# Threshold attention and a SwiGLU block: the first planned slots, six products by blocks and the order of the last jobs

## Chip, cores and metric

One Trainium2 chip, one of its cores. The metric is the device time of one execution in microseconds (us). The kernel before was timed three times: 1342.71, 1343.5 and 1345.19, median 1343.5.

The core's engines run side by side, each through its own queue in order: TensorE (PE; PEld is its weight load), VectorE (DVE), ScalarE (ACT) and GpSimd (POOL). SyncE (SP) issues the DMA transfers.

## What is computed

Attention with a threshold, over 8 batches of 8 heads, 576 tokens and 64 columns a head, and then a SwiGLU block on the 4608 tokens by 512 columns that come out of it. All is fp32.

```python
scores = scale * np.matmul(q, k.transpose(0, 1, 3, 2))
thresh = np.max(scores, axis=-1, keepdims=True) - tau
scores = np.where(scores >= thresh, scores, -1000000000.0)
scores = scores - np.max(scores, axis=-1, keepdims=True)
attn = np.exp(scores)
attn = attn / (np.sum(attn, axis=-1, keepdims=True) + 1e-09)
x = np.matmul(attn, v)            # then (batch, seq, heads * 64) -> (4608, 512)
...
g = x @ w_gate                    # w_gate, w_val: 512 x 1536
silu = g * (1.0 / (1.0 + np.exp(-g)))
return silu * (x @ w_val) @ w_out # w_out: 1536 x 512
```

## The kernel before

**Chunks.** The 4608 tokens are nine chunks of 512: c = 0 to 7 hold the first 512 tokens of each batch, c = 8 (`B` in the code) the last 64 tokens of all batches. A chunk's gate and value are made in groups g of the columns of d_ff, each group by a Strassen-Winograd scheme: seven products p1 to p7 of half-sized matrices in place of eight, with sums of weights and sums of x made beforehand, and the products joined afterwards by sums on DVE, POOL and ACT. From chunk `DEEP` = 2 on, the output product (by w_out) is done by the same scheme on two levels (class `Deep`).

**By blocks.** A flat product is eight rows of PE's record, each 128x128 weights against 256 columns. By blocks (`NestedGroup`, L1321) it is split once more into seven block products of 128 columns, 14 rows, which need sums of x (`deepen_x`, L1305), an emptying of two banks (`Seven.fill`, L1271 and L1273) and a fold of four sums (`Seven.fold`, L1276). Groups 1, 2 and 3 of chunks 3 to 6 have two such products each, p5 and p3 (`FOLDS`, `WITH_BLOCKS`).

**Attention in slots.** After a prologue with batch 0, which ends near 129 us, the heads of batches 1 to 7 run in 84 slots s, 12 to a batch: batch b holds slots 12(b−1) to 12b−1, and kk is the number of the slot in its batch, from 0. A slot makes the scores of two heads for a third of the tokens (`slot_scores`, L2058), and `slot_rest` does the rest: row maxima on DVE (L2079, L2081), exchanged between groups of partitions by DVE (L2087) or by ACT, the negative maximum (L2088, L2097), the threshold on ACT (L2100), six exponentials on ACT (L2104), six masks with sums on DVE (L2106), the exchange of the sums on ACT (L2115), total and reciprocal on DVE (L2120, L2121), six scalings on ACT (L2133) or POOL (L2130), and three transposes on DVE (L2135). PE's next scores reuse the banks that the masks read. Every third slot ends with attend (L2157), the product by v, which waits for the transposes. Tables say which slots do a job where: `FIRST_MAX_BY_ACT` and `FIRST_POOLED` by s for batches 1 and 2, `MAX_BY_ACT` and `POOLED` by kk for the others.

**Between scores and attend** PE does other work, so many steps a slot by tables: `PLAIN` in batch 1 (the rest of chunks 0 and 1, without Strassen sums of weights; L1371), `GV` for the gates and values of chunk b−1 during batch b, `CD` and `CH` for output products. PE's order is thus written out by hand. The weights' last pieces, w_out, come in during the first slots: SP loads them, ACT splits them (L953, L956), DVE and POOL join them (`rest_of_weights`).

**The planner.** The order of DVE, ACT, POOL and SP comes from a list scheduler (class `Plan`). Each job has an engine, a duration that the code gives it (`took`), jobs it waits for, a `lag` added for its readers and a rank. Whenever an engine is free by the plan, it takes the ready job of lowest rank; -1 goes ahead of 0. The engines then run the order so found, whatever the real times are: a job that waits longer than planned holds up those behind it.

**Tail.** After the last scores (near 1110 us) no slots are left. Chunks 7 and 8 run group by group in turn (class `Whole`, from L2526; PE rows at L2543), every product by blocks; `finish` gives the tanh (L2593) and the gated sums (L2595), L2615 and L2625 empty p3 and p7 onto earlier products. Chunk 8's gated sums are stored to HBM (L2608) and loaded back at its output product (L2669). The output product of chunk 7 starts inside the last group: its sums are `early`, `sums_of_last`, `late` (all of whole blocks, through `sum`), and `inner_sums` (o) for the product o of seven, of four sums j3, j1, j2, j4 that wait for each other. `gates_end` is the step that ends the last group and calls `late` if nobody did. `p7_alone` uses the sixth inner sums. L929 and L926 are the helpers by which all sums on DVE and on POOL are recorded, L1768 and L1777 PE rows of output products, L2018 and L2020 emptying into sums, L1829 and L1642 stores of outputs and loads of weight sums.

Of the kernel before, what the change touches and what calls it, by code (L numbers as in the profile page):

```python
# [14 lines left out]
ALU = mybir.AluOpType  # L15
# [129 lines left out]
def kernel(  # L145
# [27 lines left out]
    NU3 = 3  # L173
# [1087 lines left out]
    class Seven(Buf):  # L1261
# [13 lines left out]
        def fold(self, eng, rank, *deps):  # L1275
# [7 lines left out]
            return job(eng, took, tt(y[:, 4:6], twice(6), y[:, 4:6], ALU.add), j, rank=rank)  # L1283
# [391 lines left out]
    class Deep:  # L1675
# [57 lines left out]
        def sum(self, out, a, b, op, x, *deps, rank=2):  # L1733
# [3 lines left out]
            if self.by_pool and not self.in_outputs:  # L1737
                tt, eng, took = pool_tt, "POOL", 1.3
            return job(eng, took, tt(out[:, fs], a[:, fs], b[:, fs], op), *deps, rank=rank)

        def inner_sums(self, o, a, place, ready, *deps):
# [5 lines left out]
            rank = 0 if o == 1 and self.c == B - 1 else 0 if o == 1 else 1 if o == 5 or o in (3, 6) and not tail[0] or o in (0, 6) and tail[0] or self.c == B - 2 else 2  # L1747
# [315 lines left out]
    def slot_rest(seg, t, pss, mark, pooled, max_by_act, rank):  # L2063
# [53 lines left out]
        xj = job("ACT", 0.78, exchange, *masks.values(), rank=1)  # L2117
# [5 lines left out]
        rj = job("DVE", 0.36, total, xj, rank=1)  # L2123
# [102 lines left out]
    def gates_and_values(c):  # L2226
# [5 lines left out]
        for g in range(NF2):  # L2232
            deep = c > DEEP and g in WITH_BLOCKS
# [59 lines left out]
    def block_part(b, kk):  # L2293
# [17 lines left out]
        if kk in GV:  # L2311
            if kk == 1:
                state["gv"], state["c"] = gates_and_values(c), c
                if c > DEEP:
                    deepen_x(c, *(j for js in streamed_kept.values() for j in js))
# [7 lines left out]
            if c == DEEP and kk <= len(NESTED):  # L2323
                deepen(NESTED[kk - 1], plan.t, *(j for js in plain_stores.values() for j in js), *summed)
# [13 lines left out]
    for s, (n, x) in enumerate((n, x) for n in range(len(halved)) for x in range(NU3)):  # L2338
# [6 lines left out]
        if s == 0:  # L2345
# [5 lines left out]
            plan.free.update(DVE=2.0, ACT=2.5)  # L2351
# [10 lines left out]
        at_, pooled, max_by_act = (kk, POOLED, MAX_BY_ACT) if b > DEEP else (s, FIRST_POOLED, FIRST_MAX_BY_ACT)  # L2362
# [273 lines left out]
    for g in range(NF2):  # L2636
        for c in (B - 1, B):
# [10 lines left out]
            for fn in (new.p2, new.p6, new.p3, new.p7) if old is not None else (new.p5, new.p2, new.p6, new.p3, new.p7):  # L2648
# [3 lines left out]
                if (c, g) == (B, NF2 - 1) and fn == new.p6:  # L2652
                    state["deep"].late(plan.t + plan.PIPE)
# [59 lines left out]
```

## Time and profile before

| | |
|---|---|
| median of three runs | 1343.5 us |
| the profiled execution, whole | 1344.29 us |
| its span on the core | 1342.4 us |
| granted clock of TensorE | 0.999 |
| PE, DVE, ACT, POOL busy | 99%, 81%, 67%, 69% |
| 16 DMA engines, kernel's own queue | 52.2% |
| HBM read, written | 169.08 MB, 38.01 MB |

Times are read from the span's start. In the views, "idle" in brackets is how long the engine stood still before a row, and the arrow names what it waited for. "x4" is so many instructions taken together, and the duration beside it is from the start of the first to the end of the last. PE's rows overlap: a row's duration is longer than the distance to the next, so PE's pace is read from start to start.

### The profile page before, as it was taken

Reading aid. Unit: us, or ns where it says so; the run is one execution under the profiler, and the core shown is the slowest. Engines: PE = TensorE matmul, PEld = TensorE weight load, DVE = VectorE, ACT = ScalarE, POOL = GpSimd, SP = SyncE. Lnnn points to the kernel's source line nnn. Section 1 sums busy time; section 2 is a strip of 40 time slices with the busy share of each in tenths; the row PEclk is TensorE's granted clock in tenths of the full one; section 3 lists DMA queues with packets and bytes.
Section 4 is the critical chain, followed back from the end, with each engine's and each line's share of the span. In section 5 each row is a group of like instructions: output and inputs, shape, how many; then the busy total and the mean of one; then the engine's idle time right before and its main releaser. Section 6 shows DMA issues by size and latency. Waiting matters only on the chain. (4 is left out here: it accounts for less than half of the span.)

```text
span 1342.4 us, 41686 instructions
## 1 busy us (share of the span) xinstructions
PE 1327.0 (99%) x16274; PEld 1123.1 (84%) x16274; DVE 1082.9 (81%) x2891; ACT 899.1 (67%) x2341; POOL 932.8 (69%) x1115
## 2 busy tenths in 40 slices
PE   9999999999999999999999999999999999999998
PEld 7777877787887878888888888888888889999998
DVE  7888898888887778888888887888888887667886
ACT  6888777767756677787777777777777775344300
POOL 2688497565685759857895779677976799856720
PEclk9999999999999999999999999999999999999999
DMA  8852424356557553656365746655474627565241
GB/s 180 205 188 92 85 58 134 122 150 178 154 166 220 174 167 89 208 165 219 76 201 168 232 111 187 178 168 149 115 214 146 213 68 232 158 202 183 88 169 40
DMA packets 230884, 209.81 MB, mean 156 GB/s; under 512 B 167968, under 2 KB 185376, under 8 KB 223008
## 3 DMA queue, kind: packets, MB, share of 16 engines
q1 hardware_dynamic: 226768, 206.22, 52.2%
q8 instruction: 129, 2.11, 0.7%
q10 hardware_dynamic: 3920, 0.92, 0.3%
q14 instruction: 67, 0.55, 0.1%
HBM read 169.08 MB, written 38.01 MB: 154 GB/s over the span
## 5 line engine op out<-in xcount | busy, mean ns | idle before, releaser
L2106 DVE SCALAR_TENSOR_TENSOR pall<-sc,th,pall 128x288 f32<-128x288 f32 x504 | 244.2, 513 | 42.6 <-ACT pall L2104 23.4
L2104 ACT ACTIVATE pall<-sc,nm 128x288 f32<-128x288 f32 x504 | 232.9, 498 | 35.3 <-DVE pall L2106 34.9
L2135 DVE STREAM_TRANSPOSE pall<-pall 128x576 f32<-128x576 f32 x252 | 188.3, 764 | 22.1 <-ACT pall L2133 12.1
L1138 PE MATMUL pb<-xall,big 128*128 128x256 f32 x864 | 205.8, 381 | 0.0
L2133 ACT ACTIVATE pall<-pall,ri 128x288 f32<-128x288 f32 x388 | 178.9, 527 | 27.7 <-DVE ri L2121 26.9
L926 POOL TENSOR_TENSOR big<-big 128x128 f32<-128x128 f32 (+3 forms) x214 | 158.9, 751 | 46.5 <-ACT big L1273 20.8
L1138 PEld LDWEIGHTS pb<-xall,big 128*128 128x128 f32 x864 | 161.2, 190 | 24.0 <-issue 2.2
L926 POOL TENSOR_TENSOR hall<-hall,tmp 128x512 f32<-128x512 f32 x80 | 102.3, 1279 | 95.6 <-DVE hall L1197 75.9
L2079 DVE TENSOR_REDUCE mx<-sc 128x2 f32<-128x576 f32 x168 | 125.7, 748 | 39.7 <-PE sc L2058 39.3
L2058 PE MATMUL sc<-kT,qT 64*32 64x288 f32 (+1 forms) x5376 | 145.3, 345 | 0.4 <-DVE pall L2106 0.4
L1138 PE MATMUL pa<-xall,big 128*128 128x256 f32 x576 | 137.7, 382 | 0.0
L2058 PEld LDWEIGHTS sc<-kT,qT 64*32 64x32 f32 x5376 | 96.2, 106 | 48.6 <-issue 9.3
L2157 PE MATMUL xa<-pall,vall 64*32 64x288 f32 x4032 | 129.4, 404 | 0.5 <-PE px L1768 0.4
L1138 PEld LDWEIGHTS pa<-xall,big 128*128 128x128 f32 x576 | 107.8, 190 | 17.5 <-issue 2.5
L2157 PEld LDWEIGHTS xa<-pall,vall 64*32 64x32 f32 x4032 | 75.6, 107 | 46.6 <-issue 5.0
L2130 POOL TENSOR_SCALAR pall<-pall,ri 128x288 f32<-128x288 f32 x116 | 58.2, 513 | 53.1 <-DVE ri L2121 52.8
L1138 PE MATMUL pe<-xall,big 128*128 128x256 f32 x384 | 91.4, 381 | 0.0
L2115 ACT COPY sums<-sums 32x6 f32<-32x6 f32 x336 | 66.6, 198 | 30.3 <-DVE pall L2106 25.2
L1138 PEld LDWEIGHTS pe<-xall,big 128*128 128x128 f32 x384 | 72.4, 190 | 11.1 <-ACT pall L2133 0.7
L2081 DVE TENSOR_REDUCE mx<-sc 128x1 f32<-128x288 f32 x168 | 75.0, 447 | 0.0
L926 POOL TENSOR_TENSOR hall<-hall 128x384 f32<-128x384 f32 (+2 forms) x69 | 70.0, 1028 | 0.8
L1196 ACT ACTIVATE vall<-tmp 128x512 f32<-128x512 f32 x72 | 45.1, 627 | 35.6 <-POOL tmp L926 19.0
(365 smaller groups left out, 3051.6 us busy)
## 6 DMA issues: line engine op xcount, KB each, us to landing
big<-sums_hbm SPq DMA_DIRECT2D x30, 1280.0 KB, 7.9
big<-sums_hbm SPq DMA_DIRECT2D x30, 1024.0 KB, 7.8
vall<-in_v_dram SPq DMA_DIRECT2D x112, 144.0 KB, 3.5
big<-sums_hbm SPq DMA_DIRECT2D x54, 256.0 KB, 3.6
sums_hbm<-big SPq DMA_DIRECT2D x36, 256.0 KB, 3.8
out_dram<-big SPq DMA_DIRECT2D x32, 256.0 KB, 2.8
qT<-in_q_dram SPq DMA_DIRECT2D x112, 72.0 KB, 4.0
kT<-in_k_dram SPq DMA_DIRECT2D x112, 72.0 KB, 3.0
```

The source lines that it names most:

```text
L926: return lambda: nc.gpsimd.tensor_tensor(out=out, in0=a, in1=b, op=op)
L1138: nc.tensor.matmul(ps[:, i], w[:, k_, i * P:(i + 1) * P], x[:, k_, :], start=first and i == k_ == 0, stop=True, skip_group_check=True)
L2058: nc.tensor.matmul(pss[h][(slice(g * G, (g + 1) * G), *part)], qT[hs, col:col + G], kT[hs, c * SH + keys[0]:c * SH + keys[1]], start=True, ...
L2079: rs.append(job("DVE", 0.72, lambda n=n, tile_=tile_: nc.vector.tensor_reduce(out=mx[:, n:n + 2, 0], in_=tile_[:, :, 0:SH], axis=AX.X, op= ...
L2081: rs.append(job("DVE", 0.42, lambda n=n, tile_=tile_: nc.vector.tensor_reduce(out=mx[:, n + 2:n + 3, 0], in_=tile_[:, :, SH:SH + SQ], axis ...
L2104: ej = job("ACT", 0.42, lambda x=x, n=n: nc.scalar.activation(ps[x], scs[x], AF.Exp, bias=nm[:, n:n + 1]), ej, masks.get((h, u - 1)), rank=0)
L2106: masks[x] = job("DVE", 0.45, lambda x=x, n=n: nc.vector.scalar_tensor_tensor(out=ps[x], in0=scs[x], scalar=th[:, n:n + 1], in1=ps[x], op0 ...
L2115: nc.scalar.copy(sm[g * G:(g + 1) * G, 0:m, 1], sm[o * G:(o + 1) * G, 0:m, 0])
L2130: scaled.append(job("POOL", 0.48 if seg["i"] >= 3 * NP else 0.4, lambda x=x, n=n: nc.gpsimd.tensor_scalar(out=x, in0=x, scalar1=ri[:, n:n ...
L2133: scaled.append(job("ACT", 0.46, lambda x=x, n=n: nc.scalar.activation(x, x, AF.Copy, scale=ri[:, n:n + 1]), rj, rank=rank))
L2135: seg["turned"].append(job("DVE", 0.72, lambda both=both: nc.vector.transpose(out=both, in_=both), *scaled, rank=rank))
L2157: nc.tensor.matmul(holds[a].ap()[x * G:(x + 1) * G, 0:SH].rearrange("d (i q) -> d i q", q=G), vr[rs, h, j, ds], p[rs, h, :, j, :], start=( ...
```

## The change

Six edits, all of order or place except the fourth, which replaces products:

1. `rest_of_weights`: the first load of a w_out piece is planned to land 7.6 us in, before 6.3; ACT is planned free 4.4 us into slot 0, before 2.5.
2. `FIRST_POOLED`, `FIRST_MAX_BY_ACT`: which slots of batches 1 and 2 have scalings on POOL and maxima exchanged by ACT. ACT exchanges the maxima in 10 slots, before 12.
3. `PLAIN`: one step of PE's work goes from slot 2 to slot 3.
4. Chunk 2 joins the chunks whose groups 1, 2 and 3 do p5 and p3 by blocks; the three `deepen` calls (sums for two-level output products) of that batch go from kk = 1 to 3 to kk = 4 to 6.
5. The last slot of all: exchange and total at rank -1, and two scalings on POOL.
6. Tail: each fold's last sum is planned with a lag of 0.6; `late` is called from `gates_end` and not after p6 of the last group, and its sums and the one of `second_of_s1` go to DVE, since the switch `by_pool` is gone; first inner sums have rank 1 in the tail except for chunk 7's, sixth ones of chunk 8 rank 0.

```diff
@@ rest_of_weights
-        landed = 6.3
+        landed = 7.6
@@ Seven.fold
-            return job(eng, took, tt(y[:, 4:6], twice(6), y[:, 4:6], ALU.add), j, rank=rank)
+            return job(eng, took, tt(y[:, 4:6], twice(6), y[:, 4:6], ALU.add), j, rank=rank, lag=0.6 if tail[0] else 0.0)
@@ Deep
-        by_pool = False
-
         def second_of_s1(self):
-            self.by_pool = True
@@ Deep.sum
-            if self.by_pool and not self.in_outputs:
-                tt, eng, took = pool_tt, "POOL", 1.3
@@ Deep.inner_sums
-            rank = 0 if o == 1 and self.c == B - 1 else 0 if o == 1 else 1 if o == 5 ...
+            rank = 0 if o == 6 and self.c == B else 0 if o == 1 and self.c == B - 1 else 1 if o == 1 and tail[0] else 0 if o == 1 else 1 if o == 5 ...
@@ slot_rest
-        xj = job("ACT", 0.78, exchange, *masks.values(), rank=1)
+        first = -1 if seg is halved[-1] and t == seg["tiles"][-1] else 1
+        xj = job("ACT", 0.78, exchange, *masks.values(), rank=first)
...
-        rj = job("DVE", 0.36, total, xj, rank=1)
+        rj = job("DVE", 0.36, total, xj, rank=first)
@@ gates_and_values
-            deep = c > DEEP and g in WITH_BLOCKS
+            deep = c >= DEEP and g in WITH_BLOCKS
@@ tables
-    POOLED = {0: 3, 1: 1, 2: 1, 3: 3, 4: 3, 5: 2, 6: 1, 7: 2, 8: 1}
+    POOLED = {NS: 2, 0: 3, 1: 1, 2: 1, 3: 3, 4: 3, 5: 2, 6: 1, 7: 2, 8: 1}
-    FIRST_POOLED = {0: 2, 4: 1, 5: 1, 8: 1, 9: 1, 11: 2, 12: 2, 13: 3, 15: 3, 16: 3, 17: 2, 19: 2, 20: 2, 22: 3, 23: 3}
-    FIRST_MAX_BY_ACT = (1, 3, 6, 9, 10, 11, 12, 13, 14, 18, 20, 21)
+    FIRST_POOLED = {0: 2, 4: 2, 5: 1, 6: 1, 8: 2, 10: 1, 11: 2, 12: 2, 13: 3, 16: 3, 17: 2, 18: 1, 19: 1, 20: 3, 22: 3, 23: 3}
+    FIRST_MAX_BY_ACT = (1, 2, 3, 6, 9, 11, 12, 14, 15, 21)
-    PLAIN = {0: 3, 1: 5, 2: 6, 3: 2, 4: 5, 5: 5, 6: 3, 7: 3}
+    PLAIN = {0: 3, 1: 5, 2: 5, 3: 3, 4: 5, 5: 5, 6: 3, 7: 3}
@@ block_part
-                if c > DEEP:
+                if c >= DEEP:
                     deepen_x(c, *(j for js in streamed_kept.values() for j in js))
-            if c == DEEP and kk <= len(NESTED):
-                deepen(NESTED[kk - 1], ...)
+            if c == DEEP and 4 <= kk < 4 + len(NESTED):
+                deepen(NESTED[kk - 4], ...)
@@ slots
-            plan.free.update(DVE=2.0, ACT=2.5)
+            plan.free.update(DVE=2.0, ACT=4.4)
-        at_, pooled, max_by_act = (kk, POOLED, MAX_BY_ACT) if b > DEEP else (s, FIRST_POOLED, FIRST_MAX_BY_ACT)
+        at_, pooled, max_by_act = (kk if n + 1 < len(halved) or x + 1 < NU3 else NS, POOLED, MAX_BY_ACT) if b > DEEP else (s, FIRST_POOLED, FIRST_MAX_BY_ACT)
@@ tail groups
-                if (c, g) == (B, NF2 - 1) and fn == new.p6:
-                    state["deep"].late(plan.t + plan.PIPE)
```

More of the change, by code (lines that the diff above doesn't have):

```diff
@@ L1746, in inner_sums @@
             tt, eng, took = (dve_tt, "DVE", 0.55) if tail[0] else (pool_tt, "POOL", 1.0)
-            rank = 0 if o == 1 and self.c == B - 1 else 0 if o == 1 else 1 if o == 5 or o in (3, 6) and not tail[0] or o in (0, 6) and tail[0] or self.c == B - 2 else 2
+            rank = 0 if o == 6 and self.c == B else 0 if o == 1 and self.c == B - 1 else 1 if o == 1 and tail[0] else 0 if o == 1 else 1 if o == 5 or o in (3, 6) and not tail[0] or o in (0, 6) and tail[0] or self.c == B - 2 else 2
             j3 = job(eng, took, tt(s3, a11, a21, ALU.subtract), *ready, *deps, rank=rank)
@@ L2322, in block_part @@
                     last_of_streamed(o, plan.t)
[L2323 to L2324 removed]
+            if c == DEEP and 4 <= kk < 4 + len(NESTED):
+                deepen(NESTED[kk - 4], plan.t, *(j for js in plain_stores.values() for j in js), *summed)
             if kk == LAST_GV:
```

## The prediction

> **What bounds the kernel now.** The page's first part was read first: busy time by engine.
>
> ```profile
> PE 1327.0 (99%) x16274; PEld 1123.1 (84%) x16274; DVE 1082.9 (81%) x2891; ACT 899.1 (67%) x2341; POOL 932.8 (69%) x1115
> ```
>
> TensorE (PE) is busy in 1327.0 of 1342.4 us, at a granted clock of 0.999. Nothing can be won but its 15.4 us of idle time, the time its matmuls are stretched by a wait inside a run, and matmul work itself. So the second view is the waits of PE, after the prologue (which the change leaves alone):
>
> ```profile
> PE sc L2543 <- DVE tmp L2625: 0.9, 1, 0.9
> PE px L1768 <- DVE big L929: 0.9, 1, 0.9
> ...
> PE sc L2543 <- ACT tmp L1273: 0.5, 1, 0.5
> PE xa L2157 <- PE px L1768: 0.4, 1, 0.4
> PE sc L2058 <- DVE pall L2106: 0.4, 1, 0.4
> ```
>
> Columns: us in total, times, longest. Five single waits, 3.1 us together. Each is followed into the timeline of the engine that is late. What the view does not show are runs that go on but are stretched, since each bank is waited for by itself; these are found by comparing a run with the same run elsewhere.
>
> **Batches 1 and 2 (slots 0 to 23).** ScalarE (ACT) in slot 0:
>
> ```profile
> 133.85 0.87 ACT L2104 ACTIVATE pall<-sc,nm 128x288 f32<-128x288 f32 x2
> 136.06 0.91 ACT L953 ACTIVATE wo<-xall 128x768 f32<-128x768 f32 x1 [1.34 <-DMA xall<-in_moe_w_out_dram]
> 136.88 0.88 ACT L2104 ACTIVATE pall<-sc,nm 128x288 f32<-128x288 f32 x2
> ```
>
> L953 stands between the second and third exponential and waits 1.34 us for a load; the masks on VectorE (DVE, L2106) then stand still for 1.45 us, end at 139.45, and PE's next scores wait:
>
> ```profile
> 139.07 2.14 PE L2058 MATMUL sc<-kT,qT 64*32 64x288 f32 x64 [0.38 <-DVE pall L2106]
> ```
>
> Idle 0.38, and the next run starts 2.07 us later where the same 64 rows take 1.63 elsewhere (592.15 to 593.78): 0.82 us in all. With the load planned at 7.6 and ACT at 4.4, the new order has all six exponentials, two sigmoid jobs and four sum copies ahead of L953. The six masks then take 3.16 us, as in slot 1 (145.94 to 149.10), from 134.99: done at 138.15, before the 138.69 at which PE is free. **Gain 0.8.** L953 comes some 3 us later; only the pieces of w_out wait for it, needed in the batches after.
>
> Slot 3's scores run 1.84 us (172.70 to 174.54), 0.21 over; slots 10 and 13 run 0.13 and 0.16 over. In all three the masks of the slot before end just as the scores begin (margins −0.07, 0.01, −0.01). The change moves half a gate product (four matmuls, eight rows of 216 ns, 1.73 us) from slot 2 to slot 3, which takes slot 2's margin of 3.31 us to about 1.6 and gives slot 3 as much. Two slots fewer have their maxima copied by ACT: eight ACT copies (L2115's like are 0.2 us) go, DVE gains some nine small reductions (0.15 to 0.17 us); POOL gets one scaling more (0.51 each). These are cheap on average (1.6 us of DVE in 148), but margins in 8 of 24 slots are 0.3 to 0.5 us, and the spread moves one 0.5 us job in about half of them. Bounds: none of them tips (+0.5 gained), or four tip by 0.2 (−0.3 net). I take 0.3 of the 0.5, less 0.1: **gain 0.2**, range −0.3 to 0.5.
>
> **Third chunk, six products by blocks.** A flat product is eight rows, by blocks 14 half rows with sums beside them. From PE's timeline, the flat one in batch 3, then one by blocks in batch 4:
>
> ```profile
> 439.58 1.89 PE L1138 MATMUL pe<-xall,big 128*128 128x256 f32 x8
> 441.31 1.89 PE L1138 MATMUL pb<-xall,big 128*128 128x256 f32 x8
> ```
>
> ```profile
> 584.38 0.61 PE L1333 MATMUL pe<-xall,big 128*128 128x128 f32 x4
> ...
> 585.94 1.89 PE L1138 MATMUL pb<-xall,big 128*128 128x256 f32 x8
> ```
>
> Start to start: 441.31−439.58 = 1.73 against 585.94−584.38 = 1.56. Whole slots agree: 13.14, 12.19 and 13.93 us for the three that hold two such products flat (batch 3), 12.81, 11.86 and 13.60 by blocks (batch 4): 0.33 three times, **0.99 us**. Per row that is 216 and 112 ns. The Trainium skill, "TensorE: Matmul & The Clock Gate", section "Back-to-back issue gap", speaks against it: weight load and matmul together set the spacing, 81 ns at 128 columns and 131 at 512; drawn between them (an estimate, 98 at 256), 14 short rows would cost 1.13 us and eight long 0.78, so the change would lose some 2 us here. The rows of this trace differ: the spacing halves with the columns.
>
> What it costs beside PE: per group two sets of folds (four POOL sums, 0.73, 0.73, 0.46, 0.73), fills on ACT (0.46 and 0.59 in place of one), four DVE sums of x, and 12 POOL sums of the two-level output products (1.0 each) are put three slots later. POOL's load in the last four slots of batch 3 (columns PE, PEld, DVE, ACT, POOL):
>
> ```profile
> 497.00:509.70 12.70, 12.70 (x80) 10.74 (x72) 11.63 (x32) 9.63 (x27) 11.94 (x13) 1.00 0.24 56
> 509.70:522.00 12.30, 12.30 (x258) 9.96 (x250) 9.31 (x25) 8.82 (x25) 11.86 (x11) 1.00 0.33 104
> 522.00:533.00 11.00, 11.00 (x163) 10.36 (x141) 9.39 (x33) 7.41 (x23) 10.92 (x13) 1.00 0.33 54
> 533.00:544.50 11.50, 11.50 (x152) 10.69 (x150) 9.29 (x26) 8.52 (x22) 11.42 (x12) 1.00 0.89 257
> ```
>
> POOL is full from the ninth slot on, so added work there runs over into batch 4: I count 4 us later for the first inner sums of its output products. They stand idle for 2.98 us there now, two shorter gaps add 0.9, and the tightest product that uses them has 1.5 us to spare. If that cover is gone, up to 0.9 us of wait. Give-back 0 to 0.9, taken at 0.15. **Gain 0.85**, range 0.1 to 1.0.
>
> **Last scores.** After the last masks (1120.49) the sums are ready at 1121.35, but DVE does L2018 and L2020 first (1121.78 to 1122.93), so ACT's six scalings end at 1125.94 and PE's attend (L2157) waits 0.42 us and is stretched by 0.24. Rank −1 for exchange and total puts L2120 and L2121 ahead; two of six scalings go to POOL, free from 1121.90. Transposes end near 1125.2, PE asks at 1126.27: 0.66 gone. L2018 and the sums behind it come 0.4 later, and POOL's queue 1.0; margins there are about 0.4. **Gain 0.45**, range 0.1 to 0.7.
>
> **Tail groups.** Each fold has four sums; the change tells the planner that the last ends 0.6 later, since the planner thought it done when it isn't:
>
> ```profile
> 1165.22 0.63 ACT L2593 ACTIVATE qT<-big 128x512 f32<-128x512 f32 x1 [1.81 <-POOL big L926]
> 1165.76 0.47 ACT L1271 ACTIVATE tmp<-sc 128x384 f32<-128x384 f32 x1
> 1166.13 0.59 ACT L1273 ACTIVATE tmp<-sc 128x512 f32<-128x512 f32 x1
> ```
>
> The tanh L2593 waits 1.81 us for POOL, with L1271 and L1273 queued behind it, which empty the bank PE needs: 0.53 idle and 0.27 of stretch. In the new order L2593 stands behind both in every tail group. Next late would be the tanh's own readers on DVE; I see none due within a product's time (1.56) of it. **Gain 0.85** with 0.13 at 1245.1, range 0.5 to 1.0.
>
> **Last group.** PE at 1271.9 waits 0.94 us for L2625, which stands behind
>
> ```profile
> 1270.15 1.57 DVE L929 TENSOR_TENSOR big<-hall,big 128x384 f32<-128x384 f32 x1
> ...
> 1271.65 1.14 DVE L2625 SCALAR_TENSOR_TENSOR tmp<-sc,tmp 128x512 f32<-128x512 f32 x2
> ```
>
> Such a sum takes 0.56 us with POOL idle (1309.33) and 1.57 beside POOL's. In the new order it stands behind L2625, whose second operation then ends at 1270.2 to 1271.6, before PE asks. **Gain 0.95**. Five late sums of 512 columns go from POOL (1.26 to 1.58) to DVE (0.68, 3.4 us together) and behind all gates. New on PE's path: the seventh product's last block needs j4 of the sixth inner sums, now behind those; ready at 1281.4 to 1283.3, wanted at 1282.0. **Loss 0.3**, range 0 to 1.3.
>
> **Last output chunk.** PE at 1312.5 waits 0.91 us for DVE, stretched by 0.26 more. DVE had stood idle for a load:
>
> ```profile
> 1295.74 1.03 DVE L929 TENSOR_TENSOR big<-xall 128x384 f32<-128x384 f32 x2 [5.86 <-DMA xall<-hall_hbm]
> ```
>
> SP issued it at 1289.26, behind the store of an output that waited for a sum until 1288.26. With the late sums behind, that sum is done by 1281 to 1283; the load lands near 1290, and rank 0 puts the sixth inner sums ahead: ready near 1302.5, wanted at 1308.3. **Gain 1.1**, range 0 to 1.2. What follows the last matmul (1338.8 to 1342.4) stays.
>
> **Sum**: 0.8 + 0.2 + 0.85 + 0.45 + 0.85 + 0.95 − 0.3 + 1.1 = 4.9 us. The profiled execution took 1344.29 around its span of 1342.4, 0.79 over the median of three; one gap of about 0.8 us near 1061.5 without a releaser is only chance in it. So the sum is taken off the median: 1343.5 − 4.9 = **1338.6**. About 0.2%, 2.7 us, is what a measurement here can tell from no change.
>
> **Rivals.**
> 1. *New waits for old* (0.22). The seventh product's block waits 1.3 instead of 0.3, slots 2 and 3 tip by 0.4, and the last attend's wait is given back by DVE's chain behind it (0.45): 4.9 − 1.85 = 3.05, 1340.5. For it: margins of 0.3 to 0.5 in many slots, DVE at 81%. Against it: each touches another place, so all three need bad luck.
> 2. *The third chunk gives all back* (0.13): POOL's four full slots push the inner sums past 1.5 us, 0.9 of wait and nothing left of 0.85, up to 0.5 more: 1339.5 to 1340. That short rows are not cheaper is in it with 0.02: the nearest rows then give 0 for 0.99, 1339.6; the page's spacing speaks for it, the products by blocks of this trace against it.
> 3. *It doesn't do what it says* (0.04): the load lands later than planned still, and L953 holds something else up in slot 0 or 1: 0.8 less, 1339.4.
> 4. *Slower: DVE bounds the tail* (0.06). DVE is busy without a gap from 1261 to 1290. If its sums keep the pace of 1.2 to 1.6 us beside POOL, the five late sums are 6.4 us, all ahead of j4 and the sums that release the last loads. Then the seventh product waits 6.4 − 1.3 = 5.1, the last loads come 2 later than before, the 0.95 and 1.1 are lost and 0.3 is replaced: 4.9 − 2.05 + 0.3 − 5.1 − 2 = −4, 1347.5. It decides from about 4.4 us of added DVE time; against it: five POOL sums fewer are what made DVE slow.
>
> **Chances.** Forecast 0.55 (gains of 3.6 to 6.2). Faster: 0.55, 0.14 of rival 1, 0.11 of 2, 0.03 of 3, together 0.83; within 0.2%: 0.08, 0.02, 0.01 and 0.01 of 4, 0.12; slower 0.05. The low end is all terms at their better bounds (0.3, 0.15, 0.25, 0.15, 0.3 and 0.1, 1.25 together) and 0.8 more, by which the lowest of the three runs lies under their median: 1336.5. The high end is rival 1 with the third chunk's 0.85 gone and 0.5 more: 4.9 − 1.85 − 0.85 − 0.5 = 1.7, 1341.8.
>
> **What would show it.** Right: L953 behind six exponentials; PE's waits on L2625, on L1273, on L929 near 1312 and on L1768 gone; six more products at L1333, in batch 3, and slots 0.33 shorter; the last load issued near 1283. Wrong: a PE wait on `xall` L929 near 1282, sc runs over 1.63 us in slots 2 to 12, a wait of pe, pa or py products in batch 4 on POOL's sums, or DVE idle for hall_hbm near 1295 again.

## The result: slower by 0.16%, with 5.1 us won and more lost elsewhere

| | before | after |
|---|---|---|
| median of 22 runs each, us | 1343.33 | 1345.15 |
| lowest and highest, us | 1342.12, 1345.89 | 1343.17, 1351.8 |
| profiled execution, its span, us | 1344.29, 1342.4 | 1346.88, 1345.1 |
| granted clock in it | 0.999 | 0.997 |

The ratio after to before is 1.0016, 95% interval 1.0009 to 1.0022: slower by 1.8 us, where 4.9 us less was predicted. The time lies outside the predicted range of 1336.5 to 1341.8. Line numbers of after are four or five lower than those of before from the slots on: L2539 is L2543 of before, L1763 is L1768, L1772 is L1777, L2053 is L2058, L1824 is L1829.

**Where it went.** PE's rows come in nearly the same order in both traces, so the same row can be looked up in both and the starts subtracted. Each step of the difference is one place:

| row of PE | before, us | after, us | difference | what lies between |
|---|---|---|---|---|
| scores of slot 0 | 128.81 | 129.81 | +1.00 | a dip of the clock in the prologue |
| scores of slot 2 | 150.81 | 150.94 | +0.13 | edit 1: −0.87 |
| scores of slot 24 | 395.99 | 395.72 | −0.27 | edits 2 and 3: −0.40 |
| scores of slot 26 | 422.18 | 422.36 | +0.18 | scores of slot 25, 2.07 us in place of 1.63: +0.45 |
| scores of slot 36 | 544.52 | 545.15 | +0.63 | edit 4: +0.45 |
| scores of slot 78 | 1049.89 | 1050.54 | +0.65 | nothing |
| scores of slot 83 | 1110.45 | 1110.30 | −0.15 | the gap of before near 1061.5, gone: −0.80 |
| px behind the last attend | 1131.47 | 1131.91 | +0.44 | edit 5: −0.66 won, 1.25 lost |
| pb, first tail group | 1141.06 | 1142.57 | +1.51 | a new wait: +1.07 |
| pb, 1200 | 1200.15 | 1200.86 | +0.71 | fold lag: −0.80 |
| px, first rows | 1275.85 | 1275.37 | −0.48 | L2625's wait gone: −1.20 |
| px, next products | 1289.07 | 1292.87 | +3.80 | the wait for j4: +2.52, a halved clock: +1.76 |
| px, last part | 1316.19 | 1318.82 | +2.63 | last load: −1.17 |

The edits won 0.87 + 0.40 + 0.66 + 0.80 + 1.20 + 1.17 = 5.1 us. Against it stand 0.45 + 1.25 + 1.07 + 2.52 + 1.76 = 7.05. Three more differences belong to these two executions and not to the change: the dip (1.00), the gap (−0.80) and the long scores of slot 25 (0.45), which e1 and e5, with the same program as far as the tail, do in 1.63 us. With them the sum is 2.6, and the spans differ by 2.7; without them it is 1.95, and the medians differ by 1.8.

The first part of the page of after, by engine. PE is busy 2.1 us longer, so part of the loss is not idle time:

```profile
PE 1329.1 (99%) x16310; PEld 1124.5 (84%) x16310; DVE 1098.6 (82%) x2916; ACT 901.2 (67%) x2339; POOL 943.5 (70%) x1129
```

PE's waits in after (us in total, times, longest), without those of the prologue. None of before's five is left; three others are there:

```profile
PE px L1763 <- DVE xall L929: 2.3, 1, 2.3
...
PE pa L2539 <- ACT pb L2553: 0.9, 1, 0.9
...
PE xa L2153 <- issue: 0.5, 1, 0.5
```

**What went as predicted.** ACT in slot 0: the six exponentials (L2099) now run ahead of the w_out piece (L953), which waits for nothing:

```profile
134.86 0.88 ACT L2099 ACTIVATE pall<-sc,nm 128x288 f32<-128x288 f32 x2
136.55 0.94 ACT L2099 ACTIVATE pall<-sc,nm 128x288 f32<-128x288 f32 x2 [0.82 <-DVE pall L2101]
...
140.44 0.95 ACT L953 ACTIVATE wo<-xall 128x768 f32<-128x768 f32 x1
```

The next scores run 1.64 us (139.63 to 141.27) and wait for nothing. The stalls at 1166 and 1272 and the one before the last output rows went too.

**The largest loss.** PE at the end of chunk 7's output product:

```profile
1281.40 1.50 PE L1763 MATMUL px<-big,xall 128*128 128x128 f32 x12
1285.26 1.59 PE L1763 MATMUL px<-extra,xall 128*128 128x128 f32 x6 [2.35 <-DVE xall L929]
1286.64 6.40 PE L1772 MATMUL py<-wo,hall 128*128 128x256 f32 x24
```

The last block of the seventh product waits 2.35 us for j4, where 0.3 was predicted with a range of 0 to 1.3; from start to start the rows ahead of it take 2.52 us more than in before. DVE ahead of j4, and j4 itself, which is the third of these rows:

```profile
1280.20 2.96 DVE L929 TENSOR_TENSOR big<-hall,big 128x512 f32<-128x512 f32 x3
1283.09 1.64 DVE L929 TENSOR_TENSOR big<-big,px 128x256 f32<-128x256 f32 x4
1284.65 0.55 DVE L929 TENSOR_TENSOR xall<-big,xall 128x384 f32<-128x384 f32 x1
```

j2, on which j4 waits, had ended at 1276.32. Three of the late sums and a combine of four sums stand directly ahead of it: 4.4 us.

And behind the wait the clock falls. The granted clock of after in four stretches (us, PE's busy time and rows, PEclk, DMA share, GB/s):

```profile
1283.00:1286.00 3.00, 0.74 (x4) 0.89 0.30 108
1286.00:1287.00 1.00, 1.00 (x5) 0.50 1.01 249
1287.00:1288.00 1.00, 1.00 (x4) 0.50 1.30 341
1288.00:1290.00 2.00, 2.00 (x9) 0.81 0.91 278
```

At 0.50 PE does half the rows: they follow each other at 427 ns, at 1.00 at 216. The six rows behind the wait take 1.38 us to the next row's start where before they took 0.67, and the 24 rows of L1772 take 6.23 where before they took 5.18. That is 0.71 + 1.05 = 1.76 us that no view of waits shows. The halved time, worked out from the means of the four stretches, is 0.66 + 2 + 0.76 = 3.4 us, and half of that is lost: 1.7. Of after's 22 executions, five have a mean clock of 1.0 (median 1344.03 us) and nine one of 0.997 (median 1346.88 us). The Trainium skill, "TensorE: Matmul & The Clock Gate", sections "What's actually happening" and "HAM oscillation — how this bites in real kernels", says that the clock is halved after an idle window of about 3.4 us, in windows that run by themselves, and advises no idle gap above that. The length agrees with this trace; the trigger does not, as PE had stood still for 2.35 us only. Here the measurement decides.

### The profile page after: what moved, and what is told of

The parts are those of the page before. It is cut to its first block, busy times and chain, and to the rows that moved or that the text cites. A ratio compares the mean times of both kernels' runs of the same rounds, so it can differ in the third digit from the quotient of the medians.

```text
span 1345.1 us, 41770 instructions
## 1 busy us (share of the span) xinstructions
PE 1329.1 (99%) x16310; PEld 1124.5 (84%) x16310; DVE 1098.6 (82%) x2916; ACT 901.2 (67%) x2339; POOL 943.5 (70%) x1129
## 4 chain that ended last, share of the span: by engine, by line
PE 89%; POOL 4%; DVE 4%; DMA 1%; issue 1%; ACT 0%; SPq 0%; ACTq 0%; DVEq 0%; POOLq 0%
PE pb L1138 14%; PE sc L2053 10%; PE px L1763 10%; PE pa L1138 9%; PE xa L2153 9%; PE po L1446 6%; PE pe L1138 5%; PE sc L2539 5%; PE pe L1333 4%; PE pb L2539 3%; PE py L1763 3%; PE pg L1371 2%; PE pv L1371 2%; PE pa L2539 2%; PE py L1772 2%; POOL big L926 1%
## 5 line engine op out<-in xcount | busy, mean ns | idle before, releaser
L2099 ACT ACTIVATE pall<-sc,nm 128x288 f32<-128x288 f32 x504 | 233.2, 498 | 40.0 <-DVE pall L2101 39.8
L926 POOL TENSOR_TENSOR big<-big 128x128 f32<-128x128 f32 (+3 forms) x230 | 170.7, 751 | 62.0 <-ACT big L1273 23.8
L2053 PE MATMUL sc<-kT,qT 64*32 64x288 f32 (+1 forms) x5376 | 145.6, 345 | 0.0
L2053 PEld LDWEIGHTS sc<-kT,qT 64*32 64x32 f32 x5376 | 95.3, 106 | 49.3 <-issue 9.8
L1138 PE MATMUL pe<-xall,big 128*128 128x256 f32 x336 | 80.1, 381 | 0.0
L926 POOL TENSOR_TENSOR tmp<-tmp 128x256 f32<-128x256 f32 (+3 forms) x53 | 51.3, 978 | 29.1 <-DVE tmp L2611 12.1
L1138 PEld LDWEIGHTS pe<-xall,big 128*128 128x128 f32 x336 | 63.3, 190 | 9.9 <-ACT xlast L2165 0.9
L1196 ACT ACTIVATE vall<-tmp 128x512 f32<-128x512 f32 x72 | 45.1, 626 | 36.1 <-POOL tmp L926 20.8
```

The lines of the kernel that those rows point to most:

```text
L926: return lambda: nc.gpsimd.tensor_tensor(out=out, in0=a, in1=b, op=op)
L1138: nc.tensor.matmul(ps[:, i], w[:, k_, i * P:(i + 1) * P], x[:, k_, :], start=first and i == k_ == 0, stop=True, skip_group_check=True)
L2053: nc.tensor.matmul(pss[h][(slice(g * G, (g + 1) * G), *part)], qT[hs, col:col + G], kT[hs, c * SH + keys[0]:c * SH + keys[1]], start=True, ...
L2099: ej = job("ACT", 0.42, lambda x=x, n=n: nc.scalar.activation(ps[x], scs[x], AF.Exp, bias=nm[:, n:n + 1]), ej, masks.get((h, u - 1)), rank=0)
```

## The experiments

**Theory.** The gains are there, and four places that the forecast priced too low or not at all take them back: j4 behind late sums (with the clock behind it), a store behind loads near 1138, masks made late by the fold sums of the third chunk, and a stop of PE's own instructions in the last attend. **Rivals**: DVE is simply too full in the tail, so that putting j4 ahead moves the wait elsewhere at the same price; the third chunk's loss comes from the `deepen` sums put three slots later; the wait near 1138 is made by the tail and not by the last slot. Each experiment ran beside runs of before on its own chip; ratios are against those.

### e1: j4 ahead of the late sums

```diff
@@ Deep.inner_sums (on after), fourth sum
-..., tt(s4, a12, s2, ALU.subtract), j2, rank=rank)
+..., tt(s4, a12, s2, ALU.subtract), j2, rank=0 if o == 6 and self.c == B - 1 else rank)
```

> The changed kernel with one job moved: j4 of chunk 7's sixth inner sums gets rank 0, which puts it right behind j2 and ahead of the late sums and the combine. Theory (j4's place makes PE wait 2.35 us near 1282.6 and be stretched by 0.9, and the clock granted at half for some 2.8 us after that wait costs 1.06 more): all three go, 4.3 us, less what is late next, 0.3: near 1341 where the changed kernel has 1345.2, and no row of the flat product behind it at 427 ns. Rival (DVE as a whole is late there, so the wait moves to the next reader of a late sum): 1 to 2 us at most, near 1344.

Measured: 1343.91 us, ratio 0.9994 (0.9986 to 1.0003), against 1.0016 with j4 late. PE in the same place:

```profile
1283.14 5.42 PE L1772 MATMUL py<-wo,hall 128*128 128x256 f32 x24 [1.28 <-DVE big L929]
```

And DVE, the four sums of the combine behind the late sums:

```profile
1281.81 1.64 DVE L929 TENSOR_TENSOR big<-big,px 128x256 f32<-128x256 f32 x4
```

The block of px no longer waits. The flat product behind it waits 1.28 us, though not for the late sums, which have ended by 1281.89: PE goes on 0.14 us after the third sum of the combine, at 1283.00. The clock stays at 1.00 through it, and L1772's rows take 5.26 us again. So the order of DVE was the cause, and some 3 us of 4.3 come back, not all: what is late next costs 1.3. That much of the rival holds.

### e2 and e3: the third chunk

e2 makes the third chunk's products flat again, with the `deepen` calls where they were:

```diff
@@ gates_and_values, block_part (on after)
-            deep = c >= DEEP and g in WITH_BLOCKS
+            deep = c > DEEP and g in WITH_BLOCKS
...
-                if c >= DEEP:
+                if c > DEEP:
...
-            if c == DEEP and 4 <= kk < 4 + len(NESTED):
-                deepen(NESTED[kk - 4], ...)
+            if c == DEEP and kk <= len(NESTED):
+                deepen(NESTED[kk - 1], ...)
```

> The changed kernel with chunk 2 flat again and its two-level sums back at kk 1 to 3. Theory (products by blocks save 0.99 us, but slots 27 and 30, whose masks come too late, and the attend between them lose 1.27): 0.3 us faster than the changed kernel, and the scores of slots 28 and 31 at 1.63 us again. Rival (by blocks gains its 0.99 and the stalls there have another cause): 1.0 us slower.

Measured: 1347.15 us, ratio 1.0020 (1.0012 to 1.0028). In batch 3 it did what the theory said: the scores of slots 28 and 31 take 1.63 us, and from slot 0 to slot 36 the kernel is 0.5 us ahead of the one by blocks (414.81 against 415.34 us). The 0.5 of idle issue in the last attend is gone too. Yet the time is no better, since the wait of pa near 1138 grew from 0.9 to 2.2 us, with the clock at 0.53 and 0.61 for four us behind it. Counted from the last slot's scores, that wait ends at nearly the same time in both kernels (30.97 us in e2, 30.61 in after), but PE, without the stop in the last attend, is there 0.88 us earlier. The stop had hidden part of the wait, so their two prices, 1.25 and 1.07, are not independent.

e3 keeps the blocks and undoes only the last hunk above.

> The changed kernel, chunk 2 still by blocks, only the three sets of POOL sums for two-level products back at kk 1 to 3. Theory (in slots 27 and 30 the folds on DVE take 0.73 to 1.11 where batch 4 has 0.42, and the folds on POOL start late, because those POOL sums run beside and ahead of them): both stalls go, about 1.2 us faster than the changed kernel, and POOL late in other slots. Rival (the folds alone fill POOL and DVE): stalls stay within 0.3 us.

Measured: 1346.61 us, ratio 1.0011 (1.0002 to 1.0020). The rival falls: from slot 0 on, batch 3 takes 0.8 us more than in after. The stall in slot 31 goes, but slot 28's scores start 1.16 us later behind the attend ahead of them, 0.95 of it idle, and slot 30 takes 0.54 more, with a wait of 0.32 for a load. The early `deepen` sums and the new fold sums then meet in the same slots. So putting them later was needed; it wasn't the loss.

What the loss is can be read from DVE. First after, slot 27 (first product by blocks of batch 3), then before, slot 39, the same place in batch 4, both between masks:

```profile
442.07 1.88 DVE L929 TENSOR_TENSOR big<-big 128x256 f32<-128x256 f32 x2 [0.34 <-ACT big L1273]
...
444.30 0.95 DVE L929 TENSOR_TENSOR big<-big 128x128 f32<-128x128 f32 x1
```

```profile
587.24 0.88 DVE L929 TENSOR_TENSOR big<-big 128x256 f32<-128x256 f32 x2 [0.30 <-ACT big L1273]
...
588.48 0.29 DVE L929 TENSOR_TENSOR big<-big 128x128 f32<-128x128 f32 x1
```

The same three sums take 2.83 us and 1.17. Of the six folds of a batch the table `FOLDS` gives POOL four and DVE two, and this is one of DVE's. POOL in after, at the same time:

```profile
441.52 2.13 POOL L926 TENSOR_TENSOR wo<-wo 128x384 f32<-128x384 f32 x2
```

A sum of 512 columns follows at 443.83. The two of this row are the last sums of weights for the two-level output products, which batch 3 alone makes there; the `deepen` sums that edit 4 moved start only at 469.68. In batch 4 POOL stands idle from 586.35 to 588.61. So DVE's sums are long where POOL works beside them; no run takes POOL's sums away from this slot alone. Masks stand behind them in DVE's queue, so the scores of slot 28 are stretched:

```profile
447.56 2.14 PE L2053 MATMUL sc<-kT,qT 64*32 64x288 f32 x64
```

The next row starts at 449.63, 2.07 us later where 64 such rows take 1.63: 0.44. With slot 31's scores (484.89 to 487.17, 0.65 over), 0.19 in attend and 0.1 near 508 that is 1.4 us against 0.99 saved. In slot 31 the fold of POOL stands behind `deepen` sums and starts 0.6 us later than in batch 4, ACT's L1196 waits 0.51 for a sum of POOL behind it, and exponentials queue behind that.

### e4: the last slot as it was

```diff
@@ slot_rest, tables (on after)
-        first = -1 if seg is halved[-1] and t == seg["tiles"][-1] else 1
+        first = 1
...
-    POOLED = {NS: 2, 0: 3, ...
+    POOLED = {0: 3, ...
```

> The changed kernel with the last slot as before: exchange and total at rank 1 and all six scalings on ScalarE. Theory (the new order of the SP queue puts loads ahead of an output store, so that a buffer comes free 1.0 us late near 1138 and PE waits 0.92 us for it): that wait goes, the wait at the last attend (0.42, with stretches 1.0 in the first kernel) comes back, net 0.0 to 0.3 faster. Rival (the wait near 1138 comes from elsewhere, such as chunk 2's sums): it stays, and the kernel is 0.7 slower.

Measured: 1346.49 us, ratio 1.0013 (1.0004 to 1.0021). The wait near 1138 is gone and attend's 0.42 us is back. So the third rival falls: the last slot makes that wait, ten us later. The time doesn't show it, because the idle issue in attend grew to 1.67 us in this kernel.

### e5, e6, e7: the parts of the change alone

e5 takes back, in after, the late sums (`by_pool`, and `late` called after p6):

```diff
@@ Deep, Deep.sum, tail groups (on after)
+        by_pool = False
...
+            self.by_pool = True
...
+            if self.by_pool and not self.in_outputs:
+                tt, eng, took = pool_tt, "POOL", 1.3
...
+                if (c, g) == (B, NF2 - 1) and fn == new.p6:
+                    state["deep"].late(plan.t + plan.PIPE)
```

> The changed kernel with the five late sums back on GpSimd and called after p6 of the last group, as before; the fold's lag and the new ranks of inner sums stay. Theory (the late sums on DVE hold up j4 and the flat product's sums; the ranks alone had taken L2625's wait away): the waits near 1283 (2.35, or 1.28 with j4 moved) go, L2625 does not wait again, and the halved clock behind goes: 4 to 5 us faster than the changed kernel, a ratio to the kernel before near 0.998. Rival (the sums beside GpSimd take 1.5 us again and L2625's 0.94 and the last load's 0.91 come back): 2 to 3 us faster, ratio near 0.9995.

Measured: 1342.97 us, ratio 0.9992 (0.9984 to 1.0001). No wait near 1283, and none for L2625 either; 1.1 us near 1138 and 0.3 of idle issue in attend are left. In this company the move of the late sums to DVE was not needed for either of the gains that the forecast booked there; e8, below, shows that it is in another.

e6 is before with edits 1 to 3 alone (`landed`, ACT's start, the three tables).

```diff
@@ rest_of_weights, slots, tables (on before)
-        landed = 6.3
+        landed = 7.6
...
-            plan.free.update(DVE=2.0, ACT=2.5)
+            plan.free.update(DVE=2.0, ACT=4.4)
...
-    PLAIN = {0: 3, 1: 5, 2: 6, 3: 2, 4: 5, 5: 5, 6: 3, 7: 3}
+    PLAIN = {0: 3, 1: 5, 2: 5, 3: 3, 4: 5, 5: 5, 6: 3, 7: 3}
```

> The kernel before with the edits of batches 1 and 2 alone (landing 7.6, ScalarE free at 4.4, the three tables). Theory: 1.2 us less, as the two traces show between the first slot's scores and 365 us (0.86 in slot 0, 0.41 in slots 2 to 13), ratio 0.9991. Rival (the gain is lost again in later slots whose plan moves with it): 0 to 0.4 us less.

Measured: 1342.61 us, ratio 0.9990 (0.9981 to 0.9999), 1.3 us with an interval of 0.1 to 2.6, where the two terms measured in after's trace are 0.87 + 0.40. The 0.40 is the same in every trace with these tables. Part of the 0.87 is luck of before's execution: from slot 0 to slot 2 it took 22.00 us, while e7, e11 and e12, with the same old order there, took 21.47, 21.77 and 21.57. Against the 21.13 of after the gain is 0.34 to 0.87.

e7 is before with the lag of the fold's last sum alone.

```diff
@@ Seven.fold (on before)
-            return job(eng, took, tt(y[:, 4:6], twice(6), y[:, 4:6], ALU.add), j, rank=rank)
+            return job(eng, took, tt(y[:, 4:6], twice(6), y[:, 4:6], ALU.add), j, rank=rank, lag=0.6 if tail[0] else 0.0)
```

> The kernel before with the fold's lag of 0.6 in the tail alone. Theory: the wait on L1273 near 1166 goes with its stretch, 0.7 us, ratio 0.9995; all other waits stay. Rival (the later tanh moves the gated sums, and L2625 in the last group is later by some tenths): 0.3 us or less.

Measured: 1345.29 us, ratio 1.0006 (0.9997 to 1.0015): no gain. PE's waits in the tail:

```profile
PE sc L2543 <- DVE tmp L2625: 1.5, 1, 1.5
PE px L1768 <- DVE big L929: 1.4, 1, 1.4
```

The stall at 1166 is gone, but two waits that before had at 0.94 and 0.91 us are longer by 0.5 each. PE came earlier to places where DVE was late anyway: in after the other edits of the tail go with it, the two waits are not there, and the 0.8 us at 1166 stay won. Which of those edits does it was not tried.

### e8, e9, e10: versions without the losing edits

e8 is after with the edits of e2, e4 and e5. e9 has e1's edit in place of e5's. e10 is e8 with chunk 7's first inner sums not ahead:

```diff
@@ Deep.inner_sums (on e8)
-            rank = ... else 0 if o == 1 and self.c == B - 1 else 1 if o == 1 and tail[0] else ...
+            rank = ... else 1 if o == 1 and tail[0] else ...
```

> The changed kernel without the parts that lost: chunk 2 flat, its two-level sums at kk 1 to 3, the last slot as before, late sums on GpSimd after p6. Theory: the terms that were seen to gain are left, 1.2 (batches 1 and 2), 0.7 (fold lag), 1.0 (L2625) and up to 1.2 (last load): 3 to 4 us under the kernel before, ratio 0.997 to 0.998. Rival (the gains were there only with the late sums on DVE): 2 us, ratio 0.9985.

> The changed kernel with chunk 2 flat, the last slot as before, and j4 of the sixth inner sums ahead; the late sums stay on VectorE. Theory (with the late sums on VectorE L2621 stays in time, and what is left of the tail is the flat product's wait for a late sum, 1.3 us): ratio to the kernel before 0.998 to 0.9985, waits on L929 near 1283 of 1.3 us and none on L2621. Rival (the fetch of PE's instructions or the store near 1138 costs it again): ratio 0.9995.

> The version that was ahead so far (chunk 2 flat, last slot as before, late sums on GpSimd), with the first inner sums of chunk 7 at rank 1, so that they stand behind L2626, for which PE waited 1.44 us there. Theory (L2626 stood behind a sum of 1.57 us beside GpSimd's, the second of the sums taken ahead of it): that wait goes, 1.4 us less than that version, unless the sums are late for the product that reads them, which would show as a wait on L929 near 1276: ratio 0.997. Rival (DVE is as late with the sums behind): the wait moves to a product of the output, ratio 0.998.

Measured: e8 1341.40 us, ratio 0.9980 (0.9971 to 0.9989); e9 1341.46, 0.9978 (0.9967 to 0.9989); e10 1341.28, 0.9976 (0.9966 to 0.9986). All three beat both kernels. Each keeps one wait of 0.9 to 1.4 us in the last group: L2625's 1.4 in e8, L1772's 1.3 in e9, px behind L929 0.9 in e10. e8's wait for L2625 is not there in e5, though the tail's code is the same. Counted from the last slot's scores, PE asks for it 1.47 us earlier in e8 (160.67 against 162.14), since neither the stop in attend nor the wait near 1138 holds it up, and the second operation of L2625 ends later (162.05 against 161.25). In e9, with the late sums on DVE, and in e10, with the first inner sums behind, the wait is gone: without the two losses ahead, one of these moves is needed after all.

### e11 and e12: edits 4 and 5 alone

e11 is before with edit 4 (the diff of e2 the other way round), e12 before with edit 5 (that of e4 the other way round).

> The kernel before with edit 4 alone (chunk 2 by blocks, two-level sums at kk 4 to 6). Theory: 0.3 to 0.4 slower from slots 25 to 35 (0.99 saved, 1.3 lost in slots 27 to 31), and the last attend, where PE's instruction stream is now 72 instructions further, stands still some 0.9 with no releaser: 1.2 slower in all, ratio 1.0009. Rival (the stalls there came from the other edits' order): 0.7 to 1.0 faster, ratio 0.9994.

> The kernel before with edit 5 alone (last slot: exchange and total at rank -1, two scalings on GpSimd). Theory: the wait at the last attend goes (0.42, and 0.27 of stretch), the wait on the two copies near 1138 for a buffer whose store is issued behind loads comes (1 to 2): 0.3 to 1.3 slower, ratio 1.0002 to 1.001. Rival (that wait hangs on chunk 2's edit): 0.7 faster, ratio 0.9995.

Measured: e11 1346.58 us, ratio 1.0018 (1.0009 to 1.0027), worse than expected: slots 28 and 31 lose 0.42 and 1.03, and PE idles 1.7 us in the last attend for its own issue. e12 1348.98 us, ratio 1.0030 (1.0019 to 1.0042): the highest of the four parts that were run alone, though its interval overlaps that of e11. PE's pa there waits 4.0 us for ACT's pb, ACT for DVE, and DVE for a store to leave the buffer that it wants to write. First DVE of e12, then SP:

```profile
1140.01 1.72 DVE L929 TENSOR_TENSOR big<-big,px 128x256 f32<-128x256 f32 x4 [3.20 <-DMA out_dram<-big]
```

```profile
1132.47 0.90 SPq L1829 DMA_DIRECT2D out_dram<-big  x2
```

The stores (L1829) stand behind the load of L2400 (issued at 1129.33) and those of the weight sums, and land 5.1 and 7.0 us after their issue, where in before the stores issued at 1130.94 and 1132.3 landed after 2.2. Behind the 4 us the clock is at 0.50 from 1142 to 1146.

### e13, e15, e16, e17: which store

e15 is e9 with the new last slot (without e4's edit), e13 is e15 with the stores of chunk 7's turn put first on SP:

```diff
@@ ship (on e15)
-    ob_jobs[n] = [job("SP", 0.1, fn, j, lag=2.8)]
+    ob_jobs[n] = [job("SP", 0.1, fn, j, lag=2.8, rank=-1 if tail[0] and c == B - 2 else 1)]
```

> The kernel of e15, and the first of the two output stores of chunk 6 near 1131 goes ahead of three loads of weight sums on the SP queue; PE, VectorE, ScalarE and GpSimd have the same order. Theory (the buffer's store is late because it stands behind loads, on the queue and in the DMA engines): it is issued 1.3 earlier and lands 2 to 4 earlier, and PE's wait on the two copies is shorter by 1.5 to all of it, 1.5 to 4 us faster than e15. Rival (the wait hangs on other work of that stretch): no more than 0.3 faster.

> e9 with the last slot of the changed kernel (exchange and total at rank -1, two scalings on GpSimd). Theory: the wait at the last attend goes (0.69 with its stretch), the wait on the two copies near 1137 comes with 1 to 4 us, and where it is over 2 us the clock behind it is granted at half: 2 to 5 us slower than e9, ratio to the kernel before 0.999 to 1.001. Rival (it was the tail's other edits that made it costly): 0.7 faster than e9.

Measured: e15 1345.38 us, ratio 1.0008 (0.9999 to 1.0018), against 0.9978 for e9: the last slot's order costs some 4 us, with a wait of 1.93 near 1138. e13 1346.73, 1.0018 (1.0009 to 1.0027), the wait 3.4: the theory as put falls. SP of e13 shows why:

```profile
1132.77 0.39 SPq L1824 DMA_DIRECT2D out_dram<-big  x1
```

The store that moved, issued at 1130.73, is that of a block joined on DVE, which had ended it at 1130.71. The one that DVE waits for is this one, of a block joined on POOL, whose combine had rank 2 and came late. So e16 puts that combine ahead as well, and e17 is e16 with the tail of e10:

```diff
@@ combine on POOL (on e13)
-            ... (pool_tt, "POOL", 0.75, 0.44, 2)
+            ... (pool_tt, "POOL", 0.75, 0.44, 0 if self.c == B - 2 else 2)
```

> The kernel of e13 (chunk 2 flat, j4 ahead, the new last slot, stores of chunk 6 at rank -1), and GpSimd joins its block ahead of four inner sums, so that its store is issued ahead of five loads. Theory (the buffer that VectorE waits for is that block's, and its store lands 5 to 7 us after it is issued when it stands among the loads): DVE's wait on the store and PE's on the two copies near 1138 go, 3 to 5 us faster than e13, and 0.7 faster than e9, which keeps the old last slot: ratio to the kernel before 0.997 to 0.9978. Rival (the wait hangs on something else, or the four inner sums, 3 us later now, are waited for): as e13, or a wait on GpSimd's sums in chunk 6's products.

> The same, with the late sums on GpSimd and the first inner sums at rank 1 as in e10, which left 0.9 of waits in the tail where e9 left 1.3. Theory: ratio 0.9965 to 0.9975. Rival (as PE comes 0.7 earlier, the last group's sums are late again by as much): as e10, 0.9976.

Measured: e16 1342.18 us, ratio 0.9982 (0.9973 to 0.9991). SP of e16:

```profile
1126.41 0.39 SPq L1824 DMA_DIRECT2D out_dram<-big  x1
```

The store is issued 6.4 us earlier than in e13, ahead of the loads of L2395 (from 1130.05 on). It still lands only 7.5 us later, near 1133.9, but that is before DVE's combine at 1136.67, which waits for no store. The wait of pa is gone with attend's wait, both at once. e13 and e16 differ in this rank alone, which settles the cause. e17: 1341.22 us, ratio 0.9976 (0.9965 to 0.9987), level with e9 and e10; the fastest found is about 3 us under before.

### e14: what stops PE in the last attend

After's last attend (PE), with no other engine to blame:

```profile
1126.21 4.59 PE L2153 MATMUL xa<-pall,vall 64*32 64x288 f32 x142
1131.31 0.67 PE L2153 MATMUL xa<-pall,vall 64*32 64x288 f32 x2 [0.51 <-issue]
```

PE stands still for 0.51 us between two rows of one run. All six kernels with the third chunk by blocks do so (after, e1, e3, e4, e5, e11: 0.3 to 1.7 us), none of the flat ones. The blocks are 600 us away; they add 36 rows and as many weight loads to PE's program. Theory: PE's instructions come by DMA in blocks (the page counts 129 packets of 16 KB on the instruction queue), and 72 more put a block's border into attend, where rows follow each other at 32 ns and a block is used up fastest, while DMA is at its fullest. e14 is e9, flat, with 18 small matmuls in the prologue, 36 rows that nothing reads:

```diff
@@ run_idle (on e9), first call only
+        for _ in range(18 if first_idle[0] else 0):
+            nc.tensor.matmul(ps[:, 0:8], ones[:, 0:P], ones[:, 0:8], start=True, stop=True)
```

> The best version so far (e9: chunk 2 flat, last slot as before, j4 ahead) with 18 matmuls of 8 columns more at the start, whose result nobody reads, so that all later instructions of PE stand 72 places further. Theory (a block of instructions is fetched too late where the last attend's short rows use them up fastest and the DMA engines are full): PE stands still 0.5 to 1.7 us with no releaser in the last attend, as in the kernels with chunk 2 by blocks; with the extra rows' own time in the prologue, 1 to 3 us slower than e9. Rival (those gaps come from chunk 2's traffic): no gap there, and only the extra rows' time, 0 to 2 us.

Measured: 1347.96 us, ratio 1.0028 (1.0017 to 1.0039), of which 5.3 us are the rows themselves in the prologue. In the last attend:

```profile
1135.88 0.67 PE L2158 MATMUL xa<-pall,vall 64*32 64x288 f32 x3 [1.09 <-issue]
```

e9 runs all 144 rows without a break, e14 stands still for 1.09 us ahead of the last three. So the number of instructions ahead makes the stop, not the blocks. For the fetch speaks one thing more: in all seven kernels that stop, PE goes on 1.29 to 1.52 us after a packet of 16 KB on the instruction queue has ended (in after the packet ends at 1129.88 and PE goes on at 1131.31; in e4, at 1130.63 and 1132.15). So the theory stands, but no row shows that PE waits for that packet, and the rows of e14 also put everything behind them 5.3 us later.

## Why the prediction was wrong, step by step

- **Slot 0, 0.8: right** in the mechanism, 0.87 by the rows predicted. Part of the size is luck of before's execution: against e7, e11 and e12, with the same old order, it is 0.34 to 0.64.
- **Slots 2 to 13, 0.2: right**, 0.40, in every trace with these tables; e6 has both together at 1.3.
- **Third chunk, 0.85: wrong sign, −0.45.** The 0.99 of shorter rows came. The give-back was put on the inner sums of batch 4 and bounded by their cover, 0 to 0.9; no pe, pa or py product waited there. It fell on the masks inside batch 3, 1.4 us. The step took all the folds as POOL's, while two of the six are DVE's, and it didn't ask what POOL does to DVE sums beside it: 1.66 us more for the three of slot 27. Rival 2 had POOL as the cause, but in the last four slots and by another mechanism.
- **Last scores, 0.45: wrong, a loss.** The 0.66 came. The step followed DVE and POOL behind the edit and not SP. The store behind loads cost 1.07 in after, 1.9 and 2.2 in e15 and e2, where the stop hides none of it, and 4.0 in e12. SP's order was changed here by ranks on ACT and DVE and two scalings on POOL.
- **Tail groups, 0.85: right in size, 0.80**, with nothing at 1245; alone it is worth nothing (e7), which the sum couldn't tell.
- **Last group: L2625's 0.95 right** (1.20 to the next matching row), with some luck in after: the second operation ended at 1271.98, behind the forecast 1270.2 to 1271.6, but PE asked 0.56 us later than in before, at 1272.47. e9 has the gain without that help. **`p7_alone`, −0.3 with a range to 1.3: the term that failed most**, −2.52 for the wait alone. The step saw j4 behind five late sums and took them at 0.68 us each, with j4 done at 1281.4 to 1283.3. It was done at 1285.20: the late sums started only at 1280.20, the combine of four stood ahead as well, and one sum beside POOL took 1.76. Rival 4 had this mechanism at 5.1 us and a chance of 0.06, against it that POOL had fewer sums; POOL still ran one of 512 columns there.
- **The clock, not in the sum: −1.76** behind the wait. A wait was priced at its own length.
- **Last output chunk, 1.1: right**, 1.17, though the load was issued at 1285.75 and not at 1283.
- **Not foreseen**: the stop of PE in the last attend (1.25). The dip of the clock in the prologue (1.00), the gap of before near 1061.5 (0.80), in no other of the 19 traces, and the long scores of slot 25 (0.45) belong to the executions. Nothing of the change runs ahead of 129 us, and the 18 traces with this same prologue start slot 0's scores anywhere from 128.67 to 131.75. The long scores are in six traces and not in e1 and e5; what makes them is not explained.

Predicted gains and measured ones agree to 0.3 us wherever a wait of before was to go, with the luck told above. What failed is the other half of the account, of what comes next: the wait for j4 was put at 0.3 us and was 2.52, the clock behind it at nothing and was 1.76, the third chunk's give-back at 0.15 and was 1.4, and the store behind loads (1.07) and the stop of PE (1.25) were not in the sum.

## What to carry to other kernels

A rank changed on one engine reorders all queues of a planner: compare the order of DMA issues on SP before and after, and for each store ask which instruction writes its buffer next. A wait on PE can cost more than its length: the clock took 1.76 us on top of 2.52 here, so look at the granted clock behind each new wait. A stop or a wait can also hide part of the next one, so removing it may win less than it measures. Price a sum on DVE by what runs on POOL at that time, and an edit alone as well as with the others: the lag was worth 0.8 us in one company and nothing by itself.

## What the runs showed of the chip

- **The clock halves after short waits, and length alone doesn't decide.** In the tail, waits of 2.2 (e2), 2.35 (after), 3.4 (e13) and 4.0 us (e12) have rows at 0.50 behind them, for 3.4 or 6.8 us; those of up to 1.5 (e7, e8), e11's stop of 1.7 and e15's wait of 1.93 do not. But in the prologue, near 118 us, it halved behind waits of 1.07 (after) and 1.08 us (e16) and not behind 1.09 (e2) or 1.05 (before).
- **DVE's sums are slower beside POOL's.** A sum of 384 columns on DVE takes 0.55 us alone and 1.08 to 1.57 beside POOL's.
- **Stores of 256 KB behind a burst of loads land late**: 5.1 to 7.5 us after issue (e12, after, e13, e16), against 2.1 to 3.3 for the others there.
- **PE stops with no releaser in the last attend**, for up to 1.7 us, at a place that moves with the number of instructions ahead of it, and goes on 1.3 to 1.5 us after a packet of the instruction queue has ended.
